# Softmax sums inverted for two head pairs at once and stored number by number, and the last products of the output layer ordered bank by bank

## The chip, the cores and the metric

The kernel runs on one core of one Trainium2 chip. The metric is the device time of one execution in microseconds (us); less is better. The engines are called TensorE (PE in the profile; its weight loads are the separate row PEld), VectorE (DVE), ScalarE (ACT), GpSimd (POOL) and SyncE (SP, which here only issues DMA transfers). A row of the profile such as "bank<-ident,st" names the tile written and the tiles read, with buffer numbers left out.

## What is computed

Attention with a forget gate over 8 batches, 8 heads, 576 positions and 64 numbers per head, and behind it a two-layer network over all 4608 positions with 512 features and 2048 hidden units:

```python
scores = scale * np.matmul(q, k.transpose(0, 1, 3, 2))
log_f = np.log(np.clip(f, 0.0001, 1.0))
cum = np.cumsum(log_f, axis=-1)
decay = cum[:, :, :, None] - cum[:, :, None, :]
scores = np.where(causal, -1000000000.0, scores + decay)
scores = scores - np.max(scores, axis=-1, keepdims=True)
attn = np.exp(scores)
attn = attn / (np.sum(attn, axis=-1, keepdims=True) + 1e-09)
x = np.matmul(attn, v)               # then (batch, position) x (head, number)
h = x @ w_in
g = np.maximum(h, 0.0) + alpha * np.minimum(h, 0.0)
return g @ w_out
```

What matters below is the division by the sum of each row. The kernel leaves the exponentials undivided, multiplies them with v, and scales the product by the reciprocals of the sums afterwards.

## The kernel before: tiles, stages and order

**Attention** works on 32 pairs of heads, n = 0 to 31, four for each batch. `attention(n)` (L518) makes for each of the two heads four tiles of 128 query rows (`tile`, L645) and one tile with the last 64 rows of both (`tail`, L567). Each tile is a product on TensorE (the scores), a masked minimum on VectorE, an exponential on ScalarE that also yields the sum of its row (`expo`, L547), a set of transposes on TensorE (L562, L686) and a copy out of the PSUM bank on ScalarE. Pairs 0 to 7 (`n < NN`) take plain fp32 products, which read the tiles q and k. Pairs 8 to 31 take products of split operands, which read QA, QB, KA, KB, X and Y; those are prepared by loads on SyncE, rounding copies on VectorE (L433) and differences on GpSimd (L499, L504).

The nine row sums of a pair stand in nine columns of a small tile `st` of 128 partitions by 28 columns: one sum per query row, so that queries run along the partitions. The values, however, are computed with queries along the free axis (64 numbers of each head on the partitions). So the reciprocals must be turned around and spread over 64 partitions. `quotients` (L625) does this for one pair: ScalarE adds the epsilon (L629), VectorE takes the reciprocal (L630), TensorE transposes the nine columns into nine rows (L632), ScalarE copies them to the tile R (L633), SyncE stores R in DRAM as 1152 numbers in a row (L638), and three transfers on SyncE (L640) read them back, each number repeated over 64 partitions, into the tile `ri`. Only pair 3 stays on the chip: `quick` (L610) spreads R by products with a selection matrix.

The values, `prods_of` (L696), multiply the transposed exponentials with v. Pairs below `NV2` do this alone (`values`, L714), as a small part (r = 0) and a large part (r = 1). From pair `NV2` on, an even pair puts its values aside in the list `waiting`, and the odd pair that follows does both in one run of products (L759 to L774). `rest` (L727) then calls `quotients`, multiplies values and reciprocals on VectorE (L733), splits the result into two parts (L735 on ScalarE, L737 on GpSimd) in a tile of `xx`, and stores the last 64 positions (L741).

**The first layer** (`ffn1`, L786) runs for each batch over 16 blocks of hidden units, 12 products of 512 columns per block (rows "bank<-xx,wi"); ScalarE and VectorE copy the bank to one of four buffers `hs` (L803, L806, L808), and SyncE stores it (L810). A ninth call takes the last 64 positions of all batches. **The second layer** (`ffn2`, L976) runs over 18 units of 256 positions. A unit has eight chunks of the hidden axis in four groups of two, seven block products per chunk (`PRODS`, L973), each of three products of 256 columns, which add into seven half banks of four PSUM banks over all eight chunks. At the end of a unit VectorE adds the half banks up into the four blocks of the output. For the last unit these sums are single steps: e0 (L1051, from bank 3), e1 (L1067, bank 2), e2 (L1068, bank 1), e5, e3 and e4 (L1065, banks 1, 0 and 0), and each block is stored as soon as it is there (L1075, two from SyncE, two from ScalarE). In the eighth chunk of that unit the seven products are taken bank by bank: bank 3, 2, 1, then the two halves of bank 0; the seventh chunk goes before it whole.

**What sets the order.** No loop order is left to the machine: every step is given to a planner (`Plan.run`, L120) with its engine, a cost, the steps that it needs, its buffers and a key (a due time). The planner runs a simulated clock over the five instruction streams (PE, ACT, DVE, POOL, SP), always takes the step that could start earliest, among equals that with the lowest key, and so writes out a fixed order for each engine. The keys of `ffn1` (1e6 and up) lie behind those of attention, so products of the first layer fill what attention leaves free on TensorE. A transfer is planned with a size `kb`, at 220 KB per us on one channel. On the chip each engine runs its list in order and waits with semaphores.

Of the kernel before, what the change touches and what calls it, by code (L numbers as in the profile page):

```python
# [24 lines left out]
NN = 8  # L25
NV2 = 8
# [157 lines left out]
def attention_moe(  # L184
# [27 lines left out]
    rd = [dram.tile([9 * 128], F32, name=f"rd{i}") for i in range(3)]  # L212
# [42 lines left out]
    rR = ring(sp, 2, [9, 128], F32, "R")  # L255
# [262 lines left out]
    def attention(n):  # L518
# [25 lines left out]
        lo, su = (lambda: bst.t[:, 0:10]), (lambda: bst.t[:, 10:19])  # L544
        sums = []

        def expo(bt, w, col, key, deps):  # L547

            ex = op("ACT", c_exp(w), lambda: ac.activation(bt.t[:, :w], bt.t[:, :w], AF.Exp, bias=lo()[:, col : col + 1], scale=-1.0,  # L549
                                                           accum_out=su()[:, col : col + 1]), key, deps, [bt, bst])  # L550
            sums.append(ex)
            return ex
# [57 lines left out]
        def quick(bR, r_, key):  # L610
# [4 lines left out]
            def prods():  # L615
                for i in range(4):
                    mm(at(128 * i), sel[:, i], bR.t, True, True)
                mm(at(512), sel[:, 4], bR.t[:, 0:64], True, False)
                mm(at(512), sel[:, 5], bR.t[:, 64:128], False, True)
# [5 lines left out]
        def quotients(key):  # L625

            bT, bR = Buf(rT), Buf(rR)

            q_ = op("ACT", 230, lambda: ac.activation(su(), su(), AF.Identity, bias=eps), key, sums + [o_eps], [bst])  # L629
            q_ = op("DVE", 190, lambda: ve.reciprocal(su(), su()), key, [q_], [bst])  # L630
            q_ = op("-", 400, lambda: None, key, [q_])
            t = op("PE", 109, lambda: pe.transpose(bT.t[0:9, 0:128], su(), ident), key, [q_, o_id], [bT, bst])  # L632
            r_ = op("ACT", c_act(128), lambda: ac.activation(bR.t, bT.t[0:9, 0:128], AF.Copy), key, [t], [bT, bR])  # L633
            if hurry:
                quick(bR, r_, key)
                return
            d = rd[n % 3]
            st_ = op("SP", 350, lambda: sy.dma_start(d.rearrange("(c q) -> c q", q=128), bR.t), key, [r_], [bR], kb=5)  # L638
            for o, (c0, c1), s0 in ((0, (0, S), 0), (64, (512, S), S), (64, (0, 512), S + 64)):
                ri_ops.append(op("SP", 350, lambda o=o, c0=c0, c1=c1, s0=s0: sy.dma_start(  # L640
                    bri.t[o : o + 64, c0:c1], d[s0 : s0 + c1 - c0].rearrange("(o s) -> o s", o=1).broadcast_to([64, c1 - c0])),
                    key, [st_], [bri], kb=(c1 - c0) / 4))
        e1, be = [None, None], [{}, {}]
# [83 lines left out]
        def rest():  # L727
            quotients(k0 + 11 - hurry)
# [25 lines left out]
        elif n % 2 == 0:  # L754
            waiting.append((prods_of, copy_v, v_deps, bT1, bT2 + [bT4], bv, rest))
            return
        else:

            prods1, copy1, deps1, bT1_, bT2_, bv_, rest1 = waiting.pop()  # L759
# [14 lines left out]
            copy_v(1, bP2, 0, st, p2)  # L774
            rest1()
# [200 lines left out]
    def ffn2(u):  # L976
# [6 lines left out]
        for g in range(NW // GW):  # L983
# [45 lines left out]
            for cc in range(GW):  # L1029
                c = GW * g + cc  # L1030
                seen = set()
                parts = (PRODS[:3], PRODS[3:])
                if u == UNITS[-1] and c == NW - 1:
                    parts = (PRODS[:1], PRODS[1:6:4], PRODS[3:5], PRODS[2:3], PRODS[6:])
                for part in parts:
                    def prods(part=part, c=c, cc=cc, bgh=bgh):
                        for ia, ib, bank, half in part:
                            o = bo[bank].t[:, 256 * half : 256 * half + 256]
                            for n, (ka, kb) in enumerate(((0, 0), (0, 1), (1, 0))):
                                first = c == 0 and n == 0 and bank not in seen  # L1040
                                seen.add(bank)
                                end = c == NW - 1 and n == 2 and (bank == 3 or (ia, bank) in ((6, 0), (4, 1), (5, 2)))
                                mm(o, bgh.t[:, ka, ia, cc], wot[c][:, kb, ib], first, end)
# [87 lines left out]
```

## Time and profile before

| what | value |
|---|---|
| time, median of 3 runs | 1086.16 us (1085.57 to 1086.74) |
| the profiled execution's own time | 1085.87 us |
| its span, first to last instruction | 1084.1 us |
| PE, PEld, DVE busy | 1078.0, 933.7, 748.3 us |
| ACT, POOL busy | 686.0, 255.8 us |
| packets and bytes of all DMA | 115920, 183.58 MB |

The span stands for 1084.1 us of the 1085.87 us of that execution; 1.8 us lie around it. "Busy" is time in which at least one instruction of the engine ran; matmuls are pipelined, so the durations of neighbours overlap. In the rows of groups, "x32 | 8.8, 274 | 0.0" means 32 instructions, 8.8 us busy in all, 274 ns mean duration, and 0.0 us in which the engine stood idle just before them. In the timeline a row has its start, its length, the engine, the line, the operation, the tiles and the number of instructions merged into it. A wait such as "PE bank L562 <- ACT e L549: 0.2, 1, 0.2" gives the waiting instruction, what released it, the total in us, how often, and the longest.

### The profile page before, as it was taken

The page shows a single profiled execution, that of the slowest core. Times are in us where ns is not written, and L with a number is a line of the kernel's source. Part 1 is how long each engine was busy: PE and PEld are TensorE (multiplying, and loading weights), DVE is VectorE, ACT ScalarE, POOL GpSimd, SP SyncE. Part 2 cuts the span into 40 slices and gives each one's busy share as a digit, 9 for nine tenths or more (in the row PEclk, how much of TensorE's full clock was granted, in tenths as well). Part 3 has the DMA queues.
Part 4 walks back from the last instruction along what each step waited for, and adds up shares of the span by engine and source line. Part 5 has one row for each costly group of instructions (what it writes and reads, how often), then busy time and mean ns, then how long its engine had stood idle before and what let it go on. Part 6 is the DMA issues. An engine that isn't in the chain of part 4 may idle for free.

```text
span 1084.1 us, 20791 instructions
## 1 busy us (share of the span) xinstructions
PE 1078.0 (99%) x7235; PEld 933.7 (86%) x7235; DVE 748.3 (69%) x1741; ACT 686.0 (63%) x1630; POOL 255.8 (24%) x349
## 2 busy tenths in 40 slices
PE   9999999999999999999999999999999999999998
PEld 5776788888888888888887888899999999999998
DVE  6778764555555554555533885669988898989994
ACT  6878696778667767776843574556455554646551
POOL 3224855354436426434402000000000000000000
PEclk9999999999999999999999999999999999999999
DMA  6657876677767676776613665363443433443411
GB/s 151 168 162 218 257 207 206 208 207 187 238 194 218 194 223 184 232 212 200 178 70 111 245 209 198 137 211 120 140 134 117 155 118 118 140 134 124 148 60 39
DMA packets 115920, 183.58 MB, mean 169 GB/s; under 512 B 18076, under 2 KB 66995, under 8 KB 115816
## 3 DMA queue, kind: packets, MB, share of 16 engines
q1 hardware_dynamic: 115400, 181.99, 55.5%
q8 instruction: 57, 0.93, 0.4%
q14 instruction: 47, 0.39, 0.1%
q10 hardware_dynamic: 416, 0.27, 0.1%
HBM read 116.89 MB, written 49.19 MB: 153 GB/s over the span
## 4 chain that ended last, share of the span: by engine, by line
PE 98%; DMA 1%; SPq 0%; POOL 0%; ACT 0%; DVE 0%; issue 0%; DVEq 0%; POOLq 0%
PE bank L332 89%; PE bank L562 8%; DMA c<-e 0%; PE bank L632 0%; PE bank L686 0%; SPq L454 0%; ACT e L549 0%; DMA q<-c 0%; POOL q L373 0%; POOL k L374 0%; POOL mask L382 0%; POOL mask L386 0%; DVE hs L1065 0%; DVE hs L1068 0%; DVE hs L1067 0%
## 5 line engine op out<-in xcount | busy, mean ns | idle before, releaser
L332 PE MATMUL bank<-xx,wi 128*128 128x512 f32 x1728 | 424.0, 395 | 0.0
L332 PEld LDWEIGHTS bank<-xx,wi 128*128 128x128 f32 x1728 | 317.3, 188 | 63.3 <-issue 0.4
L808 DVE SCALAR_TENSOR_TENSOR hs<-bank,sa,hs 128x512 f32<-128x512 f32 x96 | 71.9, 749 | 94.6 <-ACT hs L806 94.3
L332 PE MATMUL bank<-wot,xx 128*128 128x256 f32 x1008 | 123.9, 283 | 0.0
L332 PE MATMUL bank<-wi,xx 128*128 128x256 f32 x1008 | 123.9, 283 | 0.0
L332 PEld LDWEIGHTS bank<-wot,xx 128*128 128x128 f32 x1008 | 122.3, 192 | 0.0
L332 PEld LDWEIGHTS bank<-wi,xx 128*128 128x128 f32 x1008 | 122.3, 192 | 0.0
L558 ACT ACTIVATE eT<-bank 128x384 f32<-128x384 f32 x240 | 108.1, 486 | 17.1 <-PE bank L562 13.2
L549 ACT ACTIVATE e<-e,st 128x512 f32<-128x512 f32 (+2 forms) x160 | 109.4, 687 | 14.1 <-DVE st L591 8.4
L504 POOL TENSOR_TENSOR KB<-rk,KA 64x288 fp32r<-64x288 f32 x96 | 80.1, 853 | 122.8 <-DVE KA L433 52.9
L806 ACT ACTIVATE hs<-bank,ab 128x512 f32<-128x512 f32 x96 | 65.9, 686 | 59.8 <-PE bank L332 59.2
L332 PE MATMUL bank<-eT,vr 128*64 128x320 f32 (+4 forms) x896 | 91.3, 359 | 0.0
L332 PEld LDWEIGHTS bank<-eT,vr 128*64 128x64 f32 x896 | 58.4, 137 | 37.0 <-issue 3.6
L664 DVE CUSTOM_DVE_ANT_0 e<-bank,mask 128x512 f32<-128x512 f32 (+1 forms) x128 | 75.2, 618 | 18.6 <-PE bank L332 15.9
L737 POOL TENSOR_TENSOR xx<-xs,xx 128x256 fp32r<-128x256 f32 x64 | 48.9, 787 | 164.0 <-ACT xx L735 156.0
L499 POOL TENSOR_TENSOR QA<-rq,QA 64x304 fp32r<-64x304 f32 x96 | 81.9, 884 | 16.3 <-DVE QA L433 14.5
L562 PE MATMUL bank<-ident,e 128*128 128x128 f32 x576 | 83.2, 273 | 0.2 <-ACT e L549 0.2
L332 PE MATMUL bank<-KA,QA 128*128 128x288 f32 (+4 forms) x288 | 82.8, 329 | 0.0
L562 PEld LDWEIGHTS bank<-ident,e 128*128 128x128 f32 x576 | 69.0, 140 | 16.0 <-issue 2.4
L664 DVE CUSTOM_DVE_ANT_0 es<-bank,mask 128x256 f32<-128x256 f32 (+1 forms) x128 | 41.7, 352 | 50.5 <-PE bank L332 43.5
L1024 ACT ACTIVATE xx<-gx 128x1024 fp32r<-128x1024 f32 x48 | 50.8, 1058 | 30.2 <-PE bank L332 13.1
L549 ACT ACTIVATE es<-es,st 128x256 f32<-128x256 f32 (+1 forms) x128 | 57.0, 447 | 12.8 <-DVE st L664 9.6
(142 smaller groups left out, 1660.6 us busy)
## 6 DMA issues: line engine op xcount, KB each, us to landing
hd<-hs SPq DMA_DIRECT2D x144, 256.0 KB
wx<-hd SPq DMA_DIRECT2D x47, 512.0 KB
rq<-in_qq_dram SPq DMA_DIRECT2D x24, 608.0 KB
rk<-in_kk_dram SPq DMA_DIRECT2D x24, 576.0 KB
hr<-hd SPq DMA_DIRECT2D x25, 512.0 KB
vr<-in_vv_dram SPq DMA_DIRECT2D x32, 320.0 KB
wr<-in_w_in_dram SPq DMA_DIRECT2D x16, 512.0 KB
wr<-in_w_out_dram SPq DMA_DIRECT2D x16, 512.0 KB
```

The source lines that it names most:

```text
L332: pe.matmul(o, lhsT, rhs, start=start, stop=stop)
L499: rdy.append(op("POOL", c_po(a1 - a0), lambda a0=a0, a1=a1: po.tensor_tensor(QA()[64:128, a0:a1], bq.t[64:128, a0:a1], QA()[64:128, a0:a1] ...
L504: rdy.append(op("POOL", c_po(a1 - a0), lambda a0=a0, a1=a1: po.tensor_tensor(KB()[0:64, a0:a1], bk.t[0:64, a0:a1], KA()[0:64, a0:a1].bitca ...
L549: ex = op("ACT", c_exp(w), lambda: ac.activation(bt.t[:, :w], bt.t[:, :w], AF.Exp, bias=lo()[:, col : col + 1], scale=-1.0, accum_out=su() ...
L558: return op("ACT", c_act(w), lambda: ac.activation(dst(), src(), AF.Copy), key, deps, [bank] + bufs)
L562: pe.transpose(t[:, c : c + 128], src[:, 128 * j : 128 * j + 128], ident)
L664: ve.tensor_tensor_reduce(out=b1.t[:, :w], in0=bS.t[:, :w], in1=mask[:, 928 - w : 928], scale=-0.125, scalar=3.0e38, op0=ALU.add, op1=ALU. ...
L737: xl = op("POOL", c_po(256), lambda r=r, t0=t0: po.tensor_tensor(bx.t[:, 1, t0 : t0 + 256], bxs[r].t[:, 0:256], bx.t[:, 0, t0 : t0 + 256]. ...
L806: cp = op("ACT", c_act(512), lambda bh=bh, bs=bs, fc=fc: ac.activation(bs.t, bh.t, AF.Relu, scale=ab[:, fc : fc + 1]), -1000, [last, o_sg] ...
L808: cp = op("DVE", c_dve(512), lambda bh=bh, bs=bs, fc=fc: ve.scalar_tensor_tensor(bs.t, bh.t, sa[:, fc : fc + 1], bs.t, ALU.mult, ALU.add), ...
L1024: his.append(op("ACT", c_acs(128 * GW * (j1 - j0)), lambda j0=j0, j1=j1, src=src, o_=o_: ac.activation(o_(0, j0, j1), src(), AF.Copy), key ...
```

## The change

Four things change.

1. From pair 6 on, an odd pair writes its nine sums beside those of the even pair before it: columns 19 to 27 of the even pair's `st`. `quotients` is called once for both, over 18 columns (epsilon, reciprocal, store), behind the odd pair's values. R and the DRAM buffers hold 18 rows.
2. From pair 8 on, the transpose L632 and the copy L633 are gone: SyncE stores the 128 by 18 reciprocals straight from `st`, in an order that makes each number of four bytes a piece of its own in DRAM, planned with kb=600. The three reads per pair stay, the even pair's first (`fetch`).
3. `NV2` goes from 8 to 6, so that pairs 6 and 7 too compute their values in one run. They keep the transpose, one of 18 columns.
4. In the last group of the last unit of `ffn2` the products go bank by bank over both chunks, seventh and eighth: bank 3 of both, bank 2 of both, bank 1 of both, then the halves of bank 0. e0 to e4 wait for the last part of their bank as before; only the indices change. For all other groups the order of the products stays as it was.

```diff
@@ -23,7 +23,7 @@
 NN = 8
-NV2 = 8
+NV2 = 6
@@ -209,7 +209,7 @@
 
-    rd = [dram.tile([9 * 128], F32, name=f"rd{i}") for i in range(3)]
+    rd = [dram.tile([18 * 128], F32, name=f"rd{i}") for i in range(3)]
@@ -252,7 +252,7 @@
     rst = ring(sp, 3, [128, 28], F32, "st")
-    rR = ring(sp, 2, [9, 128], F32, "R")
+    rR = ring(sp, 2, [18, 128], F32, "R")
@@ -541,13 +541,16 @@
         bT4, bst = Buf(rT4), Buf(rst)
-        lo, su = (lambda: bst.t[:, 0:10]), (lambda: bst.t[:, 10:19])
+
+        mate = waiting[-1] if n >= NV2 and n % 2 else None
+        bsu = mate[-1][0] if mate else bst
+        lo, su = (lambda: bst.t[:, 0:10]), (lambda: bsu.t[:, 19:28] if mate else bsu.t[:, 10:19])
         sums = []
 
         def expo(bt, w, col, key, deps):
 
             ex = op("ACT", c_exp(w), lambda: ac.activation(bt.t[:, :w], bt.t[:, :w], AF.Exp, bias=lo()[:, col : col + 1], scale=-1.0,
-                                                           accum_out=su()[:, col : col + 1]), key, deps, [bt, bst])
+                                                           accum_out=su()[:, col : col + 1]), key, deps, [bt, bst] + ([bsu] if mate else []))
             sums.append(ex)
             return ex
 
@@ -613,10 +616,11 @@
             at = lambda c0: bB[c0 // 512].t[:, c0 % 512 : c0 % 512 + (128 if c0 < 512 else 64)]
 
             def prods():
+                R9 = bR.t[0:9]
                 for i in range(4):
-                    mm(at(128 * i), sel[:, i], bR.t, True, True)
-                mm(at(512), sel[:, 4], bR.t[:, 0:64], True, False)
-                mm(at(512), sel[:, 5], bR.t[:, 64:128], False, True)
+                    mm(at(128 * i), sel[:, i], R9, True, True)
+                mm(at(512), sel[:, 4], R9[:, 0:64], True, False)
+                mm(at(512), sel[:, 5], R9[:, 64:128], False, True)
 
             q_ = op("PE", 1400, prods, key, [r_, o_sel], bB + [bR])
             for c0, c1 in ((0, 512), (512, S)):
@@ -624,22 +628,33 @@
 
         def quotients(key):
 
-            bT, bR = Buf(rT), Buf(rR)
-
-            q_ = op("ACT", 230, lambda: ac.activation(su(), su(), AF.Identity, bias=eps), key, sums + [o_eps], [bst])
-            q_ = op("DVE", 190, lambda: ve.reciprocal(su(), su()), key, [q_], [bst])
-            q_ = op("-", 400, lambda: None, key, [q_])
-            t = op("PE", 109, lambda: pe.transpose(bT.t[0:9, 0:128], su(), ident), key, [q_, o_id], [bT, bst])
-            r_ = op("ACT", c_act(128), lambda: ac.activation(bR.t, bT.t[0:9, 0:128], AF.Copy), key, [t], [bT, bR])
-            if hurry:
-                quick(bR, r_, key)
-                return
-            d = rd[n % 3]
-            st_ = op("SP", 350, lambda: sy.dma_start(d.rearrange("(c q) -> c q", q=128), bR.t), key, [r_], [bR], kb=5)
+            w = 18 if mate else 9
+            both, ready = (lambda: bsu.t[:, 10 : 10 + w]), sums + (mate[-1][1] if mate else [])
+
+            q_ = op("ACT", 230, lambda: ac.activation(both(), both(), AF.Identity, bias=eps), key, ready + [o_eps], [bsu])
+            q_ = op("DVE", 190, lambda: ve.reciprocal(both(), both()), key, [q_], [bsu])
+            d = rd[n % 3 if n < NV2 else n // 2 % 3][0 : 128 * w]
+            if n >= NN:
+                st_ = op("SP", 350, lambda: sy.dma_start(d.rearrange("(c q) -> q c", q=128), both()), key, [q_], [bsu], kb=600)
+            else:
+                bT, bR = Buf(rT), Buf(rR)
+                q_ = op("-", 400, lambda: None, key, [q_])
+                t = op("PE", 109, lambda: pe.transpose(bT.t[0:w, 0:128], both(), ident), key, [q_, o_id], [bT, bsu])
+                r_ = op("ACT", c_act(128), lambda: ac.activation(bR.t[0:w], bT.t[0:w, 0:128], AF.Copy), key, [t], [bT, bR])
+                if hurry:
+                    quick(bR, r_, key)
+                    return
+                st_ = op("SP", 350, lambda: sy.dma_start(d.rearrange("(c q) -> c q", q=128), bR.t[0:w]), key, [r_], [bR], kb=w / 2)
+            if mate:
+                mate[-1][2](key, st_, d[0 : 9 * 128])
+            fetch(key, st_, d[128 * (w - 9) : 128 * w])
+
+        def fetch(key, st_, d):
             for o, (c0, c1), s0 in ((0, (0, S), 0), (64, (512, S), S), (64, (0, 512), S + 64)):
                 ri_ops.append(op("SP", 350, lambda o=o, c0=c0, c1=c1, s0=s0: sy.dma_start(
                     bri.t[o : o + 64, c0:c1], d[s0 : s0 + c1 - c0].rearrange("(o s) -> o s", o=1).broadcast_to([64, c1 - c0])),
                     key, [st_], [bri], kb=(c1 - c0) / 4))
+
@@ -725,7 +740,6 @@
         v_deps = lambda: e1 + e2[0] + e2[1] + [e4, o_zero, l_v]
 
         def rest():
-            quotients(k0 + 11 - hurry)
@@ -752,11 +766,11 @@
             for r in range(2):
                 values(r, k0 + 9.6 - hurry)
         elif n % 2 == 0:
-            waiting.append((prods_of, copy_v, v_deps, bT1, bT2 + [bT4], bv, rest))
+            waiting.append((prods_of, copy_v, v_deps, bT1, bT2 + [bT4], bv, rest, (bst, sums, fetch)))
             return
         else:
 
-            prods1, copy1, deps1, bT1_, bT2_, bv_, rest1 = waiting.pop()
+            prods1, copy1, deps1, bT1_, bT2_, bv_, rest1, _ = waiting.pop()
             st = k0 + 9.6 - hurry
@@ -772,6 +786,8 @@
             copy_v(0, bP, 256, st, p_)
             p2 = op("PE", ns_v[1] + 60, prods_of(1, lambda: bP2.t), st, d_ + [p_], [bP2, bv] + bT2 + [bT4])
             copy_v(1, bP2, 0, st, p2)
+        quotients(k0 + 11 - hurry)
+        if n >= NV2:
             rest1()
         rest()
     w_ready = {}
@@ -1026,30 +1042,29 @@
             for h, (j0, j1, src, bb) in enumerate(((0, 1, a_, bhr), (1, 3, b_, bhr), (3, 7, s_(3, 7), bgx))):
                 rdy.append(op("DVE", c_dve(128 * GW * (j1 - j0)), lambda j0=j0, j1=j1, src=src, o_=o_: ve.tensor_tensor(
                     o_(1, j0, j1), src(), o_(0, j0, j1).bitcast(F32), ALU.subtract), key, [his[h]], [bb, bgh], two=True))
-            for cc in range(GW):
+            seen = set()
+            todo = [(cc, part) for cc in range(GW) for part in (PRODS[:3], PRODS[3:])]
+            if u == UNITS[-1] and g == NW // GW - 1:
+                todo = [(cc, part) for part in (PRODS[:1], PRODS[1:6:4], PRODS[3:5], PRODS[2:3], PRODS[6:]) for cc in range(GW)]
+            for m, (cc, part) in enumerate(todo):
                 c = GW * g + cc
-                seen = set()
-                parts = (PRODS[:3], PRODS[3:])
-                if u == UNITS[-1] and c == NW - 1:
-                    parts = (PRODS[:1], PRODS[1:6:4], PRODS[3:5], PRODS[2:3], PRODS[6:])
-                for part in parts:
-                    def prods(part=part, c=c, cc=cc, bgh=bgh):
-                        for ia, ib, bank, half in part:
-                            o = bo[bank].t[:, 256 * half : 256 * half + 256]
-                            for n, (ka, kb) in enumerate(((0, 0), (0, 1), (1, 0))):
-                                first = c == 0 and n == 0 and bank not in seen
-                                seen.add(bank)
-                                end = c == NW - 1 and n == 2 and (bank == 3 or (ia, bank) in ((6, 0), (4, 1), (5, 2)))
-                                mm(o, bgh.t[:, ka, ia, cc], wot[c][:, kb, ib], first, end)
-
-                    last = op("PE", 3 * len(part) * c_mm(256), prods, key + cc / 2 + (part[0][0] > 0) / 4,
-                              [last] + his + rdy + wo_ready[c], bo + [bgh])
-                    ends_of.append(last)
+                def prods(part=part, c=c, cc=cc, bgh=bgh):
+                    for ia, ib, bank, half in part:
+                        o = bo[bank].t[:, 256 * half : 256 * half + 256]
+                        for n, (ka, kb) in enumerate(((0, 0), (0, 1), (1, 0))):
+                            first = c == 0 and n == 0 and bank not in seen
+                            seen.add(bank)
+                            end = c == NW - 1 and n == 2 and (bank == 3 or (ia, bank) in ((6, 0), (4, 1), (5, 2)))
+                            mm(o, bgh.t[:, ka, ia, cc], wot[c][:, kb, ib], first, end)
+
+                last = op("PE", 3 * len(part) * c_mm(256), prods, key + m / 20,
+                          [last] + his + rdy + wo_ready[c], bo + [bgh])
+                ends_of.append(last)
         bs = Buf(ros)
         e0 = op("ACT", c_act(256), lambda: ac.activation(bs.t[:, 3], bo[3].t[:, :256], AF.Copy), -500,
-                [ends_of[-5] if u == UNITS[-1] else last], [bo[3], bs])
+                [ends_of[-9] if u == UNITS[-1] else last], [bo[3], bs])
 
         def ends():
             ve.tensor_tensor(bs.t[:, 0:5:4], two(bo[2].t), rep(3), ALU.add)
@@ -1064,10 +1079,10 @@
-            e1 = op("DVE", c_dve(512), lambda: ve.tensor_tensor(bs.t[:, 0:5:4], two(bo[2].t), rep(3), ALU.add), -500, [e0, ends_of[-4]], [bo[2], bs])
-            e2 = op("DVE", c_dve(512), lambda: ve.tensor_tensor(bs.t[:, 5:7], two(bo[1].t), rep(4), ALU.add), -500, [e1, ends_of[-3]], [bo[1], bs])
+            e1 = op("DVE", c_dve(512), lambda: ve.tensor_tensor(bs.t[:, 0:5:4], two(bo[2].t), rep(3), ALU.add), -500, [e0, ends_of[-7]], [bo[2], bs])
+            e2 = op("DVE", c_dve(512), lambda: ve.tensor_tensor(bs.t[:, 5:7], two(bo[1].t), rep(4), ALU.add), -500, [e1, ends_of[-5]], [bo[1], bs])
             e5 = op("DVE", c_dve(256), add(cd(3), lambda: t_(1, 0), cd(6)), -500, [e2], [bo[1], bs])
-            e3 = op("DVE", c_dve(256), add(cd(2), lambda: t_(0, 1), cd(6)), -500, [e2, e5, ends_of[-2]], [bo[0], bs])
+            e3 = op("DVE", c_dve(256), add(cd(2), lambda: t_(0, 1), cd(6)), -500, [e2, e5, ends_of[-3]], [bo[0], bs])
             e4 = op("DVE", c_dve(256), add(cd(1), lambda: t_(0, 0), cd(5)), -500, [e3, ends_of[-1]], [bo[0], bs])

```

## The prediction

> **What bounds the kernel now.** I read the head of the page first, for span, busy times and the chain that ended last by engine.
>
> ```profile
> span 1084.1 us, 20791 instructions
> PE 1078.0 (99%) x7235; PEld 933.7 (86%) x7235; DVE 748.3 (69%) x1741; ACT 686.0 (63%) x1630; POOL 255.8 (24%) x349
> PE 98%; DMA 1%; SPq 0%; POOL 0%; ACT 0%; DVE 0%; issue 0%; DVEq 0%; POOLq 0%
> ```
>
> PE is busy nearly throughout, and the chain lies on it for 98%. Busy alone does not prove a bound, since matmul durations overlap, so the second view is PE's own waits, the third the longest piece of the chain, and the fourth the rows of the tile xs, for when the last reciprocals are used.
>
> ```profile
> PE bank L395 <- DVE wbf L392: 1.5, 1, 1.5
> PE bank L332 <- DMA q<-c: 0.4, 1, 0.4
> PE bank L562 <- ACT e L549: 0.2, 1, 0.2
> 552.22 526.38 PE bank L332 x3770
> L733 DVE TENSOR_TENSOR xs<-xs,ri x64: 411/484/1132, 33.6 to 594.4; 128x256 f32<-128x256 f32 x32, 128x320 f32<-128x320 f32 x32
> ```
>
> PE waits three times in the whole program, 2.1 us together. From 552.22 on it runs 526 us without a break, and the last multiplication by a reciprocal, at 594.4, falls well inside that run. So the time is the sum of PE's instructions, plus a head that the change leaves alone, plus a tail behind the last product. An instruction taken off PE is worth its slot; one taken off another engine is worth nothing by itself; and a delay costs only when it makes PE wait.
>
> **Transposes of the sums.** The groups give the transpose by line, the timeline gives its neighbours.
>
> ```profile
> L632 PE MATMUL bank<-ident,st 128*9 128x128 f32 x32 | 8.8, 274 | 0.0
> 547.86 0.93 PE L562 MATMUL bank<-ident,e 128*128 128x128 f32 x7
> 550.01 0.60 PE L562 MATMUL bank<-ident,e 128*128 128x128 f32 x4
> 550.45 0.27 PE L632 MATMUL bank<-ident,st 128*9 128x128 f32 x1
> 550.48 1.64 PE L332 MATMUL bank<-xx,wi 128*128 128x512 f32 x6
> 551.95 0.27 PE L632 MATMUL bank<-ident,st 128*9 128x128 f32 x1
> 551.98 4.35 PE L332 MATMUL bank<-xx,wi 128*128 128x512 f32 x18
> 115.65 5.71 PE L332 MATMUL bank<-xx,wi 128*128 128x512 f32 x24
> ```
>
> 32 transposes stand in the trace, one per pair. Pairs 0 to 5 keep theirs, pairs 6 and 7 share one, and pairs 8 to 31 lose theirs: 25 go. The mean of 274 ns is not the price, as it holds the pipeline's depth too. Seven transposes in a row take 0.93 us and four take 0.60, that is 0.11 us for each further one (0.33 over 3). This is the slot of a transpose beside others. The other bound is one that breaks into the first layer's products: the 24 products from 550.48 to 556.33 with one transpose inside take 5.85 us, 24 without one take 5.71, so 0.14. I take 0.11, since most of the 25 stand beside other transposes or values: 25 x 0.11 = 2.75 us, with 3.5 us as the upper end. The lower end is nothing at all, if the slots could hide under their neighbours; the spacing speaks against that, and it is a rival below.
>
> The page "TensorE: Matmul & The Clock Gate" of the Trainium skill, section "Back-to-back issue gap", gives about 81 ns for each product of 128 columns in a sustained stream. This trace does not agree for these fp32 transposes (0.11 us); by the page the term would be an estimated 2.0 us and the sum below 3.05 us instead of 3.8.
>
> **Values of pairs 6 and 7 in one run.**
>
> ```profile
> 108.29 0.87 PE L332 MATMUL bank<-eT,vr 128*64 128x256 f32 x8
> 110.97 2.27 PE L332 MATMUL bank<-eT,vr 128*64 128x320 f32 x20
> 124.50 2.92 PE L332 MATMUL bank<-eT,vr 128*64 128x256 f32 x28
> 127.35 0.28 PE L632 MATMUL bank<-ident,st 128*9 128x128 f32 x1
> 162.85 5.63 PE L332 MATMUL bank<-eT,vr 128*64 128x320 f32 x56
> ```
>
> Pair 6 takes its 28 products in two pieces, 0.87 + 2.27 us, pair 7 in one of 2.92: 6.06 us. Two pairs in one run, as from pair 8 on, take 5.63. The difference of 0.43 counts the drain of two runs too many; a run ends 0.07 us behind the start of what follows (124.50 + 2.92 against 127.35). That leaves 0.29, so 0.3 us. The bounds are 0.21 (twice 2.92 against 5.63) and 0.43. Pair 6's values then come some 15 us later; the first layer's products stand between the pieces already and fill the place.
>
> **The tail.** The timeline of the last 15 us:
>
> ```profile
> 1069.79 10.24 PE L332 MATMUL bank<-wi,xx 128*128 128x256 f32 x84
> 1077.91 0.38 ACT L1051 ACTIVATE hs<-bank 128x256 f32<-128x256 f32 x1 [11.06 <-PE bank L332]
> 1078.68 0.69 DVE L1067 TENSOR_TENSOR hs<-bank,hs 128x512 f32<-128x512 f32 x1 [10.58 <-PE bank L332]
> 1079.48 0.69 DVE L1068 TENSOR_TENSOR hs<-bank,hs 128x512 f32<-128x512 f32 x1
> 1080.20 1.09 DVE L1065 TENSOR_TENSOR hs<-bank,hs 128x256 f32<-128x256 f32 x3
> 1080.66 1.00 ACTq L1075 DMA_DIRECT2D out_dram<-hs  x2
> ```
>
> PE ends at T = 1080.03, with 0.12 us for a product (10.24 over 84). Twelve products lie behind bank 2, so it is done at 1078.59, and e1 starts 0.09 later. VectorE is then late: e1, e2, e5, e3 and e4 run one behind the other to 1081.29, T + 1.26. With both chunks bank by bank, 24 products lie behind bank 2, 12 behind bank 1, and 6 behind the first half of bank 0. e1 then starts at T - 2.79, e2 at T - 1.35, e5 0.72 later, e3 at T - 0.3, all ahead of PE's end. Only e4 is left: from T + 0.09, about 0.4 us long, to T + 0.5. The tail shortens by 0.75 us. What is late next is the last store, from 1081.29 to the span's end at 1084.1, 2.8 us, which stays. Bounds: 0 if the four stores together set that end, 0.9 if they also land sooner for being spread out. PE's own work is the same 84 products.
>
> **What moves elsewhere.** Off PE the change removes the copies to R and their stores for 24 pairs, merges those of pairs 6 and 7, halves the epsilons and reciprocals of pairs 6 to 31 (13 fewer of each, the others twice as wide), and adds 12 stores of another kind.
>
> ```profile
> L629 ACT ACTIVATE st<-st,eps 128x9 f32<-128x9 f32 x32 | 9.5, 296 | 0.2
> L633 ACT ACTIVATE R<-bank 9x128 f32<-9x128 f32 x32 | 8.2, 256 | 12.0 <-PE bank L632 12.0
> L630 DVE RECIPROCAL st<-st 128x9 f32<-128x9 f32 x32 | 6.7, 209 | 20.3 <-ACT st L629 20.2
> L638 SPq DMA_DIRECT2D rd<-R x31: 274/302/1981, 25.5 to 552.6; - x31
> SPq L640 <- DMA rd<-R: 11.1, 7, 3.7
> q1 hardware_dynamic: 115400, 181.99, 55.5%
> q10 hardware_dynamic: 416, 0.27, 0.1%
> 300.00:400.00 100.00, 100.00 (x652) 82.27 (x650) 54.20 (x173) 74.45 (x214) 46.81 (x62) 1.00 0.71 205
> ```
>
> That takes about 25 x 0.256 + 13 x 0.296 = 10 us from ScalarE and under 3 us from VectorE; at 54% (VectorE) and 74% busy from 300 to 400 us neither holds up PE, so I count nothing. (That last row gives the busy us of PE, PEld, DVE, ACT and POOL, the clock, the DMA share and GB/s.) The even pair's reciprocals now wait for the odd pair's last exponential, one pair later; the cover is the backlog of first-layer products, which lasts beyond 594.4.
>
> The new store has 128 x 18 = 2304 pieces of four bytes, 144 for each of 16 engines if they share evenly. No row shows such pieces. On q1 a packet costs 55.5% of 16 x 1084.1 us over 115400, which is 83 ns at 1577 bytes; on q10 it is 42 ns at 650 bytes (from a rounded 0.1%). The line through the two meets four bytes at 13 ns, an estimate. So a store takes between 144 x 13 ns = 1.9 us and 144 x 83 ns = 12 us of every engine. The planner allows 600 / 220 = 2.7 us. I take the low end, as the pieces are nearer to 650 bytes than to 1577 and far below both: 12 x 1.9 = 23 us of engine time at a DMA share of 0.71, which fits. SyncE waits in line for the reciprocal, and then, ahead of the first read L640, for the landing (today up to 3.7 us of wait); queued behind it are loads (L488, L489, L496) and the first layer's stores (L810), for which the four buffers hs wait. How much lateness they bear, one pair shows:
>
> ```profile
> 432.62 0.34 SPq L488 DMA_DIRECT2D rq<-in_qq_dram  x1
> 439.80 0.48 SPq L496 DMA_DIRECT2D QB<-QA  x1
> 447.01 3.26 POOL L499 TENSOR_TENSOR QA<-rq,QA 64x304 fp32r<-64x304 f32 x4
> 450.85 0.22 PE L332 MATMUL bank<-KA,QA 128*128 128x128 f32 x1
> ```
>
> The copy QB is issued 7.2 us before GpSimd uses it. If its landing takes the 3.7 us that a read waited for one, 3.5 us are spare there; GpSimd then ends at 450.27 (447.01 + 3.26), 0.6 us before PE's first product of the pair. So some 4.1 us of lateness beyond the plan cost nothing here. I count nothing, with 0.3 us for each store as the end where the gain is used up.
>
> **Sum.** 2.75 + 0.3 + 0.75 = 3.8 us. The profiled execution has 1085.87 us, 1.8 of them around the span of 1084.1: a span of 1080.3 and a time of 1082.07. The median of the runs, 1086.16, lies 0.29 above the profiled execution: **1082.4 us**. Upper ends of all terms, 3.5 + 0.43 + 0.9 = 4.8, give 1081.4.
>
> **Rivals.** *Short waits on PE eat the gain.* PE's order is written out with planned landings; where they differ on the chip, PE stands still. A wait of 0.24 us behind each of 12 stores takes 2.9 us back: 1085.3. For it speaks the margin of 0.6 us at 450.85, against it that PE waited once, 0.2 us, in all of attention's later part.
>
> *The transposes were hidden.* If PE had had their slots free, 0.3 + 0.75 are left: 1085.1. The 5.85 against 5.71 speak against it.
>
> *The stores block the queue, and it gets slower.* At 83 ns a piece a store takes 12 us, 9.3 beyond plan; loads behind it come 5.2 us later than they can bear. If six of the 12 stores meet such a load, PE waits 31 us; the loss begins at 6.8 us a store (47 ns a piece), and I carry the middle, 15.6 us less the 3.8: 1098.0. For it speaks only that the piece has no row of its own; against it the small packets of q10.
>
> By the page "DMA: Bandwidth & Descriptors" of the Trainium skill, section "Specifications", a transfer below 512 bytes makes the engine read, modify and write, and its "Rules for kernel authors" advise against a last dimension that is not contiguous, with one descriptor for each element. This trace cannot show either; both speak for this rival.
>
> **How the numbers follow.** About 0.2%, 2.2 us, is what a measurement can tell here: below 1084.0 is faster, above 1088.3 slower. Forecast 0.66, short waits 0.20, hidden transposes 0.05, blocked queue 0.09. A fifth of the short-wait case is small enough to stay faster: 0.70 faster, 0.21 the same, 0.09 slower. The range runs from 1081.4 to 1086.4, where the waits have eaten all; outside lie the blocked queue and some 0.05 below.
>
> **What would show it.** L632 should stand 7 times, PE's waits stay near 2.1 us, the chain on PE at 98%. DMA packets should rise by about 12 x 2304 = 27,600. The last run of additions should end 0.5 us behind PE, not 1.26. I am wrong if PE waits for QA, KB, X or Y, if ScalarE waits for hs, or if packets grow much less.

## The result, and the profile after

The changed kernel takes 1133.19 us (median of 6 runs, 1129.34 to 1138.74), the kernel before 1086.36 us (1084.96 to 1087.65): a ratio of 1.0441, with a 95% interval of 1.0428 to 1.0455. It is 47 us slower, where 4 us less were forecast, and it lies outside the range.

The head of the page of the changed kernel, with the clock that was granted to PE and the busy share of the DMA engines in 40 slices, the packets, and the chain by engine; then the mean clock of the core:

```profile
span 1131.5 us, 20645 instructions
PE 1091.9 (97%) x7210; PEld 939.8 (83%) x7210; DVE 745.9 (66%) x1728; ACT 678.5 (60%) x1592; POOL 254.2 (22%) x349
PEclk9999999999998999999998999999999999999999
DMA  6657787779987978889979366646434444344421
q1 hardware_dynamic: 142799, 181.99, 64.1%
PE 48%; DMA 14%; issue 3%; ACT 2%; POOL 1%; DVE 1%; SPq 1%; POOLq 0%; DVEq 0%; ACTq 0%
```

```profile
core 0: 1131.5 us, clock 0.986
```

PE was the chain for 98% before; now it is for 48%, and DMA for 14%. PE is busier in microseconds although 25 instructions fewer run on it. The waits of PE, the whole answer:

```profile
PE bank L565 <- ACT e L552: 14.5, 8, 6.2
PE bank L332 <- POOL QA L499: 6.0, 5, 1.9
PE bank L332 <- DVE st L594: 5.7, 1, 5.7
PE bank L565 <- ACT es L552: 3.2, 2, 2.9
PE bank L332 <- DVE hs L824: 2.3, 2, 1.3
PE bank L395 <- DVE wbf L392: 1.5, 1, 1.5
PE bank L332 <- DVE st L679: 1.0, 1, 1.0
PE bank L332 <- DMA X<-QA: 0.9, 1, 0.9
PE bank L332 <- POOL xx L751: 0.2, 1, 0.2
PE bank L332 <- DMA q<-c: 0.2, 1, 0.2
```

They add up to 35.5 us, against 2.1 before. Hardly any of them names a DMA: PE waits for ScalarE, VectorE and GpSimd, which work no longer than before. What those wait for stands one step further back, in SyncE's own waits and in VectorE's:

```profile
SPq L654 <- DMA rd<-st: 99.1, 12, 12.1
```

```profile
DVE QA L433 <- DMA rq<-in_qq_dram: 39.1, 10, 7.3
DVE xs L747 <- DMA ri<-rd: 34.8, 19, 7.6
```

SyncE stands still for the landing of each of the 12 stores, 8.3 us on average. VectorE stands in line for the loads of q (6.5 us before) and for the reciprocals (15.3 before). One place shows the whole run, first SyncE's timeline, then VectorE's, then PE's, then the engines' busy times (PE first), PE's clock and the DMA share in stretches around it:

```profile
376.81 0.39 SPq L638 DMA_DIRECT2D rd<-st  x1
377.87 0.42 SPq L826 DMA_DIRECT2D hd<-hs  x1
378.88 0.33 SPq L489 DMA_DIRECT2D rk<-in_kk_dram  x1
381.51 0.32 SPq L826 DMA_DIRECT2D hd<-hs  x1
382.20 0.71 SPq L488 DMA_DIRECT2D rq<-in_qq_dram  x1
391.99 1.75 SPq L654 DMA_DIRECT2D ri<-rd  x3
```

```profile
398.00 0.86 DVE L433 CAST QA<-rq 128x608 fp32r<-128x608 f32 x2 [5.56 <-DMA vr<-in_vv_dram]
399.21 0.83 DVE L747 TENSOR_TENSOR xs<-xs,ri 128x320 f32<-128x320 f32 x2 [0.35 <-DMA ri<-rd]
```

```profile
402.43 1.97 PE L565 MATMUL bank<-ident,e 128*128 128x128 f32 x8 [4.58 <-ACT e L552]
```

```profile
398.00:402.00 4.00, 0.00 (x0) 0.00 (x0) 3.62 (x7) 2.26 (x7) 1.41 (x2) 1.00 0.85 191
402.00:406.00 4.00, 3.57 (x14) 3.20 (x15) 0.75 (x1) 3.28 (x8) 3.92 (x7) 0.57 0.53 151
406.00:410.00 4.00, 4.00 (x19) 3.33 (x18) 2.75 (x4) 1.38 (x2) 3.36 (x4) 1.00 0.83 203
```

The store is issued at 376.81, and the reads that need it only at 391.99, 15.2 us later. The load rq, issued at 382.20 while the store runs, is not used before 398.00, the load rk of 378.88 not before 400.62. (The profile puts the 5.56 us in VectorE's row down to the load of vr, issued at 393.79; the step itself reads rq.) VectorE runs nothing from 392.4 to 398.0, ScalarE waits for VectorE, and PE stops for 4.58 us. What the DMA engines moved meanwhile, in rows of the same kind (the last three numbers are PE's clock, the DMA share and GB/s):

```profile
372.00:376.80 4.80, 4.80 (x30) 4.06 (x29) 2.31 (x6) 4.60 (x14) 2.42 (x3) 1.00 0.84 219
379.50:383.50 4.00, 4.00 (x31) 2.61 (x31) 0.75 (x1) 0.69 (x1) 2.67 (x4) 1.00 0.92 23
383.50:387.50 4.00, 4.00 (x44) 2.85 (x40) 0.00 (x0) 1.39 (x4) 0.00 (x0) 1.00 0.87 29
392.00:396.00 4.00, 4.00 (x25) 3.39 (x24) 0.44 (x2) 1.96 (x6) 0.00 (x0) 1.00 1.00 348
```

With rk, rq and results of the first layer on order, 23 to 29 GB/s move while the store is on its way, at a share of about 0.9, and 348 GB/s once it has landed. So the store holds up the other transfers, and does not only come late itself.

A part of the wait is paid a second time, by the clock. It stands at 0.50 in six stretches of the span; two of them, the sum of all six, and the stop of PE that lies around the beginning of the first one shown:

```profile
350.92:357.74 6.82, 6.06 (x18) 4.90 (x19) 5.17 (x20) 4.17 (x12) 0.40 (x1) 0.50 0.98 245
402.12:405.53 3.41, 3.10 (x12) 2.81 (x13) 0.75 (x1) 3.16 (x8) 3.41 (x5) 0.50 0.50 137
sum 30.71, PE 22.41 PEld 19.74 DVE 17.57 ACT 16.69 POOL 6.57; mean PE 3.74 PEld 3.29 DVE 2.93 ACT 2.78 POOL 1.10
```

```profile
351.68 0.69 PE L565 MATMUL bank<-ident,es 128*128 128x128 f32 x2 [2.87 <-ACT es L552]
```

PE works in 22.4 of these 30.7 us; at half the clock that costs some 11.2 us. (The mean clock of 0.986 over the span would give 1131.5 x 0.014 = 15.8 us, but it also counts time in which PE stood still.)

So the 47.4 us between the two spans are about 33.4 us of added waits and 11.2 us of lower clock, less some 3.4 us that the change does save (measured below): 41.2, with some 6 us unexplained.

### The profile page after: what moved, and what is told of

It reads as the page before. It is cut to its first block, busy times and chain, and to the rows that moved or that the text cites. A ratio compares the mean times of both kernels' runs of the same rounds, so it can differ in the third digit from the quotient of the medians.

```text
span 1131.5 us, 20645 instructions
## 1 busy us (share of the span) xinstructions
PE 1091.9 (97%) x7210; PEld 939.8 (83%) x7210; DVE 745.9 (66%) x1728; ACT 678.5 (60%) x1592; POOL 254.2 (22%) x349
## 3 DMA queue, kind: packets, MB, share of 16 engines
q1 hardware_dynamic: 142799, 181.99, 64.1%
## 4 chain that ended last, share of the span: by engine, by line
PE 48%; DMA 14%; issue 3%; ACT 2%; POOL 1%; DVE 1%; SPq 1%; POOLq 0%; DVEq 0%; ACTq 0%
PE bank L332 46%; DMA rd<-st 7%; DMA ri<-rd 3%; DMA rq<-in_qq_dram 3%; PE bank L565 2%; POOL QA L499 1%; DMA Y<-KB 1%; SPq L654 1%; ACT eT L561 1%; ACT e L552 1%; DMA Z<-c 0%; DVE xs L747 0%; ACT hs L822 0%; ACT Z L479 0%; ACT xx L749 0%
## 5 line engine op out<-in xcount | busy, mean ns | idle before, releaser
L332 PE MATMUL bank<-xx,wi 128*128 128x512 f32 x1728 | 431.6, 399 | 0.3 <-POOL xx L751 0.2
L552 ACT ACTIVATE e<-e,st 128x512 f32<-128x512 f32 (+2 forms) x160 | 109.6, 688 | 29.2 <-DVE st L679 15.5
L561 ACT ACTIVATE eT<-bank 128x384 f32<-128x384 f32 x240 | 106.7, 486 | 15.8 <-PE bank L565 11.6
L332 PE MATMUL bank<-KA,QA 128*128 128x288 f32 (+4 forms) x288 | 85.3, 339 | 16.0 <-POOL QA L499 6.0
L565 PE MATMUL bank<-ident,e 128*128 128x128 f32 x576 | 86.0, 278 | 14.7 <-ACT e L552 14.5
L822 ACT ACTIVATE hs<-bank,ab 128x512 f32<-128x512 f32 x96 | 65.0, 686 | 41.2 <-PE bank L332 37.3
L499 POOL TENSOR_TENSOR QA<-rq,QA 64x304 fp32r<-64x304 f32 x96 | 80.9, 875 | 18.6 <-DVE QA L433 16.8
L332 PEld LDWEIGHTS bank<-KA,QA 128*128 128x128 f32 x288 | 54.0, 198 | 22.0 <-POOL QA L499 9.2
```

The costliest lines, as they stand in the source:

```text
L332: pe.matmul(o, lhsT, rhs, start=start, stop=stop)
L499: rdy.append(op("POOL", c_po(a1 - a0), lambda a0=a0, a1=a1: po.tensor_tensor(QA()[64:128, a0:a1], bq.t[64:128, a0:a1], QA()[64:128, a0:a1] ...
L561: return op("ACT", c_act(w), lambda: ac.activation(dst(), src(), AF.Copy), key, deps, [bank] + bufs)
L565: pe.transpose(t[:, c : c + 128], src[:, 128 * j : 128 * j + 128], ident)
L822: cp = op("ACT", c_act(512), lambda bh=bh, bs=bs, fc=fc: ac.activation(bs.t, bh.t, AF.Relu, scale=ab[:, fc : fc + 1]), -1000, [last, o_sg] ...
```

## The experiments

Lines of code are those of the changed kernel unless another one is named. The time of the kernel before was measured beside each group of runs and lay between 1085.10 and 1086.01 us.

**Only the size of the pieces.** Same plan, same instructions, 128 pieces of 72 bytes for 2304 of four, which leaves the numbers in another order in DRAM:

```diff
-  sy.dma_start(d.rearrange("(c q) -> q c", q=128), both())
+  sy.dma_start(d.rearrange("(q c) -> q c", c=18), both())
```

> The changed kernel with one difference: each store writes the 18 reciprocals of a partition as one piece of 72 bytes (128 pieces instead of 2304), so the numbers stand in DRAM in another order and the output is not the reference's; plan and instruction order are the same. Theory P (the four-byte pieces themselves hold the DMA engines for 14 us a store) and theory Q (SyncE stands still for the landing, and that alone delays the loads) both expect the landing in 3 to 4 us, SyncE's wait for it under 20 us in all instead of 99.1, PE's waits near 2 us, and 1082 to 1084 us. Theory R (the new order and the joint reciprocals of two pairs are what is slow) expects 1125 us or more.

Measured: 1082.22 us, ratio 0.9971 (0.9959 to 0.9982). This is the forecast's own number (1082.4). PE's waits, and the last products and additions:

```profile
PE bank L395 <- DVE wbf L392: 1.5, 1, 1.5
```

```profile
1066.50 10.24 PE L332 MATMUL bank<-wi,xx 128*128 128x256 f32 x84
1076.78 0.76 DVE L1080 TENSOR_TENSOR hs<-bank,hs 128x256 f32<-128x256 f32 x2 [0.29 <-PE bank L332]
```

PE waits 1.5 us in all. So the plan, its new order, and the joint reciprocals of two pairs cost nothing, and theory R falls. All of the 51 us between this kernel and the changed one hang on how the same 9 KB of a store are cut into pieces.

**The same change with the transpose kept.**

```diff
-  if n >= NN:          # the direct store
+  if n >= 99:          # never: 18 columns through TensorE for every two pairs
```

> The changed kernel with the transpose and the copy kept for all pairs (18 columns, one for two pairs), stored as 18 rows of 512 bytes. P and Q: 13 transposes fewer than before, 13 x 0.11 + 0.3 + 0.75 = 2.5 us, so 1083.9 us. R: still 1125 us or more, since two pairs share one late step.

Measured: 1083.85 us, ratio 0.9985 (0.9976 to 0.9994). Of the kernels that compute the reference's output in full this is the fastest, ahead of both. It lies 1.6 us behind the first, where 12 transposes at 0.11 us would be 1.3. That the two agree is partly luck: PE waits 2.4 us here against 1.5, and is busy for 1076.0 us against 1075.3, so 0.9 of the 1.6 us are waits.

**Reads planned later.** SyncE is to do other work while the store lands:

```diff
+  st_ = op("-", 11000, lambda: None, key, [st_])     # behind the store
```

> The changed kernel with its four-byte store, but the planner is told that the reads come 11 us later, so that it puts other transfers between store and reads on SyncE. Q: SyncE's wait for the landing falls from 99.1 us to under 25 us and the time with it, to 1090 us or less. P: SyncE waits less, but loads that are issued behind the store still land late, PE still waits 15 us or more, and the time stays above 1105 us. R: no change, 1125 us or more.

Measured: 1150.56 us, ratio 1.0599 (1.0584 to 1.0613). SyncE no longer stands still for the store ahead of the reads (21.2 us ahead of other transfers are left), and VectorE's wait for ri falls from 34.8 to 13.2 us. Its wait for rq rises from 39.1 to 63.8 us. The transfers put between store and reads now run beside the store and are late themselves. Theory Q, that SyncE's standing still is the only cause, falls.

**The end alone.** The kernel before with the last part of the diff:

> The kernel before with only the last group's products bank by bank. By the prediction's term the additions end 0.5 us behind PE instead of 1.26 and the time falls by 0.75 us, to 1085.6 us; if the four stores set the end, nothing changes.

Measured: 1084.89 us beside 1085.65, ratio 0.9994 (0.9985 to 1.0003): the expected size, but not clear of no change.

**The same pieces elsewhere, from elsewhere, and half of them.** Three kernels, edited at the store:

```diff
# e5_own_line: two transfers, i = 0 and 1, in place of one
+  sy.dma_start(d.rearrange("(q a b) -> q a b", a=9, b=2)[:, :, i], both()[:, 9 * i : 9 * i + 9])
# e6_other_queue: ScalarE's queue, and the reads planned 16 us later
+  st_ = op("ACT", 600, lambda: ac.dma_start(d.rearrange("(c q) -> q c", q=128), both()), key, [q_], [bsu])
+  st_ = op("-", 16000, lambda: None, key, [st_])
# e7_half_pieces: 9 columns in four-byte pieces, 9 in pieces of 36 bytes
+  sy.dma_start(d[0:h].rearrange("(c q) -> q c", q=128), both()[:, 0:9])
+  sy.dma_start(d[h:].rearrange("(q c) -> q c", c=9), both()[:, 9:18])
```

> The changed kernel with the same 2304 four-byte pieces per store, but the 18 of a partition stand within 72 bytes of their own (two transfers of 1152 pieces, every second number each), so neighbouring numbers in DRAM come from one partition and not from 128; the order in DRAM is not the right one, and the output is not the reference's. P-count (the number of pieces sets the price): the landing stays near 14 us and the time above 1115 us. P-place (pieces of different partitions within one stretch of 512 bytes get in each other's way): landing under 7 us, time under 1090 us.

Measured: 1188.1 us, ratio 1.0936 (1.0918 to 1.0954). Giving each partition a place of its own in DRAM does not help, which speaks for the number of pieces. That it is slower still than the changed kernel was not expected. The edit also makes two transfers of one; why it is slower is open.

> The changed kernel with the four-byte store issued from ScalarE's queue instead of SyncE's, and the reads planned 16 us later, so that SyncE neither issues the store nor stands still for it. P-ring (loads suffer because they stand behind the store in one queue of each DMA engine): SyncE's loads land in time, PE waits under 5 us, 1082 to 1088 us. P-engine (the pieces take the engines or the write path itself, whichever queue they come from): PE still waits 15 us or more, above 1110 us.

Measured: 1181.4 us, ratio 1.0882 (1.0856 to 1.0907), with 88.4 us of VectorE's waits for rq, though SyncE stands still for the store for only 6.8 us in all. (Reads planned 11 us late cost nothing by themselves, as the last experiment shows.) Stretches around the store that ScalarE issues at 344.97, and the line of the page for ScalarE's queue:

```profile
345.00:349.00 4.00, 4.00 (x24) 2.62 (x24) 0.75 (x1) 1.09 (x2) 3.14 (x4) 1.00 0.94 213
349.00:353.00 4.00, 4.00 (x48) 2.73 (x44) 0.00 (x0) 0.82 (x2) 0.00 (x0) 1.00 1.65 40
353.00:357.00 4.00, 4.00 (x26) 3.44 (x23) 1.96 (x9) 2.67 (x9) 0.00 (x0) 1.00 0.92 45
```

```profile
q10 hardware_dynamic: 28256, 0.38, 2.1%
```

Again little moves, 40 to 45 GB/s. Another queue does not shield SyncE's loads, so the order in one queue is not the cause. This queue carries nearly only the pieces (416 packets of it are others), and the profile records 0.021 x 16 x 1178.7 us / 28256 = 14 ns for one of its packets.

> The changed kernel with only 9 of the 18 columns in four-byte pieces (1152), the other 9 as one piece of 36 bytes per partition (wrong order, so the output is not the reference's). If the price is linear in the pieces, the store lands in about 8 us, near the point where the prediction's third rival begins to lose (6.8 us): 1083 to 1095 us. If there is a threshold or a fixed price of a scattered store, 1110 us or more.

Measured: 1111.37 us, ratio 1.0233 (1.0217 to 1.0248); SyncE's wait for the store falls from 99.1 to 53.0 us. Against the first experiment 128 pieces lose nothing, about half the pieces 29 us, and all of them 51. Over these three kernels the loss is near linear in the number of pieces, and there is no free half; the expected 1083 to 1095 was too low. The landing is not linear: from the store's issue to the reads 10.9 to 15.0 us pass here, where some 8 were expected, and 12.6 to 16.8 in the changed kernel.

**The planner told the price.**

```diff
-  ... [bsu], kb=600)
+  ... [bsu], kb=2700)
```

> The changed kernel unchanged in what it moves, but the planner is told 2700 KB, that is 12.3 us, for each store instead of 2.7. If the loss came from a plan that did not know the price, most of it goes: 1083 to 1095 us. If the engines simply lack the time or the loads cannot be moved, the time stays above 1110 us.

Measured: 1204.76 us, ratio 1.1092 (1.106 to 1.1123), the slowest of all. VectorE's wait for rq falls to 3.6 us, as the loads are now kept away from the store; its wait for ri rises to 74.7. PE now waits most for GpSimd's QA, 47.2 us. This plan moves the price about and does not remove it; whether another could is not shown.

**Pieces without their use, and lateness without pieces.** The kernel with the transpose, plus a store that nobody reads; and the kernel with 72-byte pieces, plus a chain of small copies behind the store:

```diff
+  op("SP", 350, lambda: sy.dma_start(x.rearrange("(c q) -> q c", q=128), both()), key, [q_], [bsu], kb=600)
```

```diff
+  at = [d[0:128], *hop, d[0:128]]          # hop: four tiles of 128 numbers in DRAM
+  for x, y in zip(at, at[1:]):
+      sy.dma_start(y, x)
```

> The kernel of e2_transpose18 (1083.85 us), with the twelve stores of 2304 four-byte pieces added at the same places, into DRAM that nobody reads; the reciprocals that are used still go through the transpose. Theory L (the loss is that the reciprocals come late, and VectorE stands in line for them): VectorE's waits for ri stay small and the time at 1083 to 1090 us. Theory E (the pieces keep the DMA engines from other transfers): VectorE waits for rq 30 us or more, and the time is above 1110 us.

Measured: 1158.45 us, ratio 1.0666 (1.0644 to 1.0689); VectorE waits 59.4 us for rq and 33.3 us for ri. Twelve stores that nothing needs cost 75 us over the kernel they were added to, and both marks of theory E are met. The run does not part the two theories wholly: SyncE stands still for these stores too, 29.2 us ahead of other transfers, and the useful store behind them is late (24.6 us of SyncE's waits ahead of its reads, against 13.1).

> The kernel of e1_pieces72 (1082.22 us; its order in DRAM is wrong and its output not the reference's), with five small copies of 512 bytes within DRAM chained behind each store, each waiting for the one before, so that the reads may start some 10 us later, with the same plan and nearly no bytes. L: time above 1105 us, VectorE's waits for ri 30 us or more. E: 1082 to 1088 us.

Measured: 1120.83 us, ratio 1.0335 (1.0313 to 1.0357). Theory E expected 1082 to 1088 here and is not the whole either. The chain does what the store's landing did: SyncE stands still for it (92.0 us in all, 47.6 at the copies from hop to hop), the reads follow the store by 10.8 to 15.1 us, the loads behind it are issued late, and VectorE waits 35.2 us for rq and 23.6 for ri. Some ten microseconds that the plan does not know of are enough for most of the loss, 38.6 of 51 us, with nearly no bytes moved.

**One store by itself.** The kernel before, with six stores of 2304 pieces added in the second layer, each read back at once by a small transfer:

> The kernel before, with six stores of 2304 four-byte pieces (of constants) added in the second layer, where the DMA share is about 0.4, each followed by a small read of it on SyncE that waits for the landing. If a piece costs the engines the same everywhere, SyncE waits 10 to 13 us for each; if the 14 us of attention are waiting behind other transfers, 2 to 5 us. The time itself is not the question.

SyncE's timeline there, and then that of the chain above, whose first part is a store in 72-byte pieces and the copy that waits for it:

```profile
813.64 0.50 SPq L1054 DMA_DIRECT2D lone<-ones  x1
827.90 0.24 SPq L1055 DMA_DIRECT2D got<-lone  x1
```

```profile
157.57 0.37 SPq L640 DMA_DIRECT2D rd<-st  x1
159.36 0.53 SPq L643 DMA_DIRECT2D hop<-rd  x1
```

14.3 us pass from issue to the read (13.6 to 14.3 over the six), in a stage with a DMA share of 0.4; 1.8 us for the same numbers in 128 pieces (1.4 to 4.1 over the twelve stores of that kernel). Around the first lone store the engines do this:

```profile
813.00:817.00 4.00, 4.00 (x36) 4.00 (x35) 3.93 (x8) 2.74 (x6) 0.00 (x0) 1.00 0.72 133
817.00:819.00 2.00, 2.00 (x19) 2.00 (x19) 1.88 (x3) 1.90 (x4) 0.00 (x0) 1.00 0.15 1
819.00:823.00 4.00, 4.00 (x36) 4.00 (x35) 3.97 (x7) 0.20 (x1) 0.00 (x0) 1.00 0.00 0
823.00:827.00 4.00, 4.00 (x35) 4.00 (x35) 3.93 (x11) 2.74 (x5) 0.00 (x0) 1.00 0.02 4
```

A load that SyncE issued 0.4 us earlier takes up the first row; behind it nothing else moves, so most of the 14 us is no waiting behind other work. With 144 against 8 pieces for each of 16 engines, if they share evenly, the landing grows by 12.5 us / 136 = 92 ns for each further piece on average. This is not time that the profile records for the pieces: for some 10 us before the read the share is between 0.00 and 0.15. What fills these 10 us the trace does not show. This kernel's one run took 1085.45 us: in the second layer, nothing is so close behind a transfer that 14 us hurt.

**Lateness that the plan knows.** The first kernel with the reads planned 11 us later, as in the third:

> The kernel of e1_pieces72 (72-byte pieces; the output is not the reference's), with the planner told, as in e3_read_later, that the reads come 11 us later, so that SyncE does other work first; nothing holds the engines. If lateness of the reciprocals alone is what the kernel cannot bear, however it is planned, the time is 1105 us or more, as in e3. If it bears planned lateness, and e3 was slow because its pieces held up the transfers that were put in between, 1082 to 1086 us.

Measured: 1081.77 us, ratio 0.9971 (0.9961 to 0.9982). Without the pieces, late reads are free if the plan knows of them. The third experiment differs from this one by the pieces alone, and takes 69 us longer.

## Why the prediction was wrong, point by point

**The failing step is the price of the new store.** "I take the low end, as the pieces are nearer to 650 bytes than to 1577", 1.9 us a store from 13 ns a piece. Measured: 14.3 us for a store by itself, and 12.6 to 16.8 us from its issue to the reads in the changed kernel. The 13 ns were not the mistake: where the pieces have a queue nearly to themselves, the profile records 14 ns for one. What failed is the product, 144 pieces times the time of a packet, as the time of a store. It gives 2 us, and some 10 us of the landing are in no packet's record. The upper end, 12 us, came near by luck, from 83 ns that these packets do not take. The sum also took the store's engine time as room beside the others (a share of 0.71, "which fits"); in fact other transfers moved at 23 to 29 GB/s while the store was on its way. Why the landing takes so long stays open.

**The third rival was what happened, and it was priced too low.** Its mechanism is right in part: loads behind the store come too late for PE, but not for the order in the queue, since a store from another queue does the same. It was carried as 1098, at a middle store of 9.4 us and with half of the stores doing harm. Three things were missing: the store took longer than its worst case; reciprocals were late as well as loads, through VectorE, which takes its steps in order; and stops of PE lowered its clock afterwards, some 11.2 us in all. The page "TensorE: Matmul & The Clock Gate" of the Trainium skill, Part 1, says that a window of about 3.4 us without work takes the clock to half, and that as long a busy window brings it back. The trace agrees in the size and the length: from 402.12, near the end of the stop of 4.58 us, the clock stands at 0.50 for 3.41 us, and at 1.00 from 406 on. It does not agree that a whole such window must be idle: at 350.92 the clock fell some 2.1 us into a stop of 2.87 us.

**Its chance, 0.09, was too small.** The text itself gave 1.9 to 12 us for an operation that no row shows, with the loss beginning at 6.8 us. About half of that span, 5.2 of 10.1 us, lay on the losing side.

**The cited advice was right.** The page "DMA: Bandwidth & Descriptors" of the Trainium skill, section "Rules for kernel authors", gives one descriptor for each element where the last dimension is not contiguous. The trace agrees: q1 carries 142799 packets for 115400, 27,399 more for 12 x 2304 = 27,648 pieces. Its limit of 512 bytes (section "Specifications") did not show as such: stores in pieces of 72 bytes landed in 1.4 to 4.1 us.

**The three terms on PE were about right.** With the store in 128 pieces the time is 1082.22 us, 3.4 us less than before in the same runs (1085.65), where 3.8 were summed. With the transpose kept it is 1.8 us less, where 2.5 were expected. The rival of hidden transposes, 1085.1, falls. Of the 3.4 us, 0.6 are waits of PE that went (2.1 us to 1.5), which the sum did not hold. PE's busy time fell by 2.7 us (1078.0 to 1075.3) where the transposes and the values give 3.05; since equal work differs by 0.6 (1077.4 with the end alone), the slot of 0.11 us fits but is not settled. The tail is the term that is a bit off: the additions end 0.80 us behind PE (1076.78 + 0.76 against 1066.50 + 10.24) where 0.5 was forecast and 1.26 stood before, because the step e3 waited for PE's end. Of the values of pairs 6 and 7 no run was made alone.

**"Some 4.1 us of lateness beyond the plan cost nothing here"** was not tested closely: the first experiment stays within it and PE waits 1.5 us, stores some 11 us beyond the plan's 2.7 us made PE wait 35.5, and no run was late by 4 to 8 us. One reading behind it is loose: GpSimd's step L499 waits for the copy QB, but it works on rq and QA and does not use QB; PE does.

## What to carry to other kernels

An operation off the bound engine is free only as long as its price is known. The packet times of a profile are no price of a transfer: what those who wait for it pay is the time from issue to landing, and here it was seven times what the packets' records gave. Where no row shows an operation, let the chance of a loss be as large as the losing share of the span. If the loss begins inside that span, a lone copy of the operation in a slack stage of the same kernel, as with the six stores here, measures it without doing harm. When PE waits for compute engines that are not busy, follow the chain one step further: the transfer behind them is named in their waits and in the issuing queue's.

## What the runs showed of the hardware that was not expected

- A store to DRAM of 2304 four-byte pieces took 13.6 to 14.3 us from issue to the read behind it in a stage with a DMA share of 0.4; for such a packet the profile records 14 ns, which is 2 us for 144 of them. Putting the pieces of one partition side by side did not lower the kernel's time (1188.1 us), nor did another queue (1181.4).
- Other transfers beside such a store were late whichever queue it came from: 23 to 29 GB/s moved, and 40 to 45 with the store on ScalarE's queue, where VectorE waited 88.4 us for loads on SyncE's.
- Stops of PE were paid a second time by the clock: from near the end of a stop of 4.58 us it stood at 0.50 for 3.41 us, in which PE worked for 3.10, some 1.6 us more. Over the changed kernel 33.4 us of added waits brought some 11.2 us of lower clock.
